# The last token tile in parts of 384 and 128 columns, wv in one transfer, and two stretches of a hand-written order dealt anew

## The chip, the cores and the metric

One core of one Trainium2 chip runs the whole kernel. The metric is device time in microseconds (us) of one execution; several executions are timed and their median is given. Engines are named as the profile names them: PE (TensorE matmul) and PEld (its weight loads), DVE (VectorE), ACT (ScalarE), POOL (GpSimd), SP (SyncE, used here only to issue DMAs).

## The reference

The input x has 2048 tokens of 512 features (bf16). It is normalised, and the result goes through an attention block A and a dense block B; the output is x + A + B.

```python
xn = layernorm(x)                                   # over 512 features, eps 1e-5
# A: 32 heads of 16, the tokens in 4 segments of 512
q, k, v = xn @ wq, xn @ wk, xn @ wv
for s in range(4):
    p = softmax(qs @ ks.T * 16 ** -0.5 + causal mask)    # within the segment
    a_dot = p @ vs
    num, den = phi(qs) @ M, phi(qs) @ z + 1e-6           # phi(t) = t + 1 if t > 0 else exp(t)
    o = g * num / den + (1 - g) * a_dot                  # g = sigmoid(beta), one for each head
    M, z = M + phi(ks).T @ vs, z + sum(phi(ks))          # memory of the segments before
A = concat(o) @ wo
# B
B = silu(xn @ w1) @ w2                              # w1 512 x 1792, w2 1792 x 512
return x + A + B
```

## The kernel before

The tokens stand in 4 segments of 4 tiles of 128. For each tile of the first segment DVE computes sums and variance (`ln_sums`, `ln_var`: words `xc`, `xd`; `xs` is both), ACT the square root (`xq`), DVE its reciprocal (`xi`) and the normalised tile (`Nv`, L315). PE transposes it (`X`, L845), and ACT or DVE copies the transposes to `xnT` (`Xa`, `Xv`, L851). In later tiles the root is taken on POOL (`xg`) and the transposes are made by DMAs that SP issues (`XD`, L857).

The projections are dense products on PE with `xnT`: `k`, `q`, `v`, and `h` for the dense block. A product of a [128, 512] result comes in parts (`v0.0.0` to `v0.0.3` for segment 0, tile 0), each one word. A copy takes the result out of PSUM (`ka`, `kv` and so on: the last letter is the engine). For the scores, k is split into two masked halves (`kf` on ACT and DVE, `kp` on POOL, L385), with masks `pm_odd` and `pm_even` that `odd` makes. `fp`, `fa`, `fv` are the steps of phi on POOL, ACT and DVE, `t` transposes phi(k) by a DMA.

Scores and exponentials go in 72 batches (`S0` to `S71`, in an order of their own: S0, S2, S1, S3, S4, S7, S5, S11, S6, S8, S9, S10, S13 are the first thirteen). One batch fills one PSUM tile `psS` of 2048 columns (L724), one ACT instruction takes the exponential to `Pb` (L730), and POOL sets the masked ones to zero (L744, "select"). `E` and `O` multiply `Pb` with v for the even and odd halves of the heads (L791). PE is a queue: what stands between two batches is worked off there while ACT runs the exp.

What runs when is set by the string `ORDER`: each word calls one function, which issues its instructions at once on their engines, so that the order of the words is the order on each engine. Semaphores between engines follow from the data. The four PSUM banks for projections and outputs are handed out in the order in which they come free.

For outputs, `out_mm` sums for one token tile the 14 products with w2 and the 4 with wo (words `o`; `oc` and `od` do half or a quarter of the columns), and `st` adds x on DVE (`o_out`, L621) and stores it. The very last token tile is summed in two column halves of its own (words `oh`, L338), and each half is added and stored by `half_store` (`sh`, `o_half`, L668 and L672), half 1 first.

The loads at the start: SP issues x tiles, wv (two transfers of 256 KB), wk, wq, more of x, w1; ACT issues two x tiles (L158).

Of the kernel before, what the change touches and what calls it, by code (L numbers as in the profile page):

```python
# [10 lines left out]
BF16 = mybir.dt.bfloat16  # L11
# [4 lines left out]
ORDER = """
ones0 ones1 zeros xc0 xd0 xc1 xq0 xi0 Nv0 busy44 xd1 xq1 xc2 busy6 xi1 X0.1 xd2 xq2 Nv1 X1.1 Xa0.1 v0.0.0 v0.0.1 v0.0.2 xs3 xi2 Nv2 xq3 xi3 v0.0.3 X2.1 Xa1.1 k0.1.0 tb Nv3 X3.1 Xv2.1 k0.1.1 Xv3.1 vv0.0 odd omask k0.0.0 k0.0.1 k0.0.2 k0.0.3 ka0.0 fp0.0 q0.0.0 kf0.0 q0.0.1 q0.0.2 q0.0.3 k0.1.2 k0.1.3 q0.2.0 v0.2.0 qa0.0 xs5 ka0.1 kp0.1
S0 v0.1.0 v0.1.1 xs6 xs7 q0.2.1 v0.2.1 v0.2.2 v0.2.3 vv0.2 fa0.0 k0.2.0 k0.2.1 k0.2.2 xs4 xg4.4
S2 q0.2.2 q0.2.3 qv0.2 k0.2.3 kv0.2 fa0.2 v0.1.2 v0.1.3 vv0.1 Nv5 Nv6 XD6 q0.1.0 q0.1.1 q0.1.2 q0.1.3 Nv7 qv0.1
S1 h0.0.0 h0.0.1 h0.0.2 fp0.2 xs10 h0.0.3 v0.3.0 v0.3.1 v0.3.2 v0.3.3 ha0.0 vv0.3 q0.3.0 hv0.0  # L20
S3 h0.3.0 h0.3.1 q0.3.1 kp0.2 q0.3.2 h0.3.2 tanh XD5 XD7 q0.3.3 h0.3.3 k0.3.0 qv0.3 k0.3.1 xs8 ha0.3
S4 Nv4 h0.1.0 k0.3.2 h0.1.1 hv0.3 XD4 h0.2.0 h0.2.1 h0.2.2 h0.2.3 ha0.2 xs9 k0.3.3 kv0.3 hv0.2
S7 xs11 xg8.4 v1.2.0 v1.2.1 v1.2.2 v1.2.3 vv1.2 h0.1.2 h0.1.3 ha0.1 E0
S5 h0.4.0 h0.4.1 hv0.1 Ev0 h0.4.2 h0.4.3 v1.1.0 v1.1.1 fv0.2 v1.1.2 v1.3.0 fp0.3 ha0.4 v1.1.3 vv1.1
S11 hv0.4 q1.2.0 q1.2.1 q1.2.2 v1.3.1 kind fa0.1 q1.2.3 qv1.2 v1.3.2 v1.3.3 vv1.3 Nv8 XD8 O0 lw0 fv0.0 Ov0
S6 fa0.3 k1.2.0 k1.2.1 k1.2.2 h0.5.0 h0.5.1 h0.5.2 q1.1.0 h0.5.3 ha0.5 kp0.3 k1.2.3 kv1.2 q1.1.1 q1.1.2 hv0.5
S8 h0.7.0 q1.1.3 qv1.1 h0.6.0 h0.6.1 h0.6.2 h0.6.3 ha0.6 kp1.2 fv0.3 E1 Ev1 k1.0.0
S9 hv0.6 h0.7.1 h0.7.2 h0.7.3 Om0 ha0.7 k1.0.1 k1.0.2 q1.0.0 q1.0.1 fp0.1 Nv9 XD9 k1.0.3 q1.0.2 kv1.0 kp1.0
S10 h0.8.0 hv0.7 xs12 h0.8.1 h0.8.2 h0.8.3 ha0.8 h0.9.0 h0.9.1 q1.0.3 t0.3 qv1.0 Nv10 XD10 h0.9.2 h0.9.3
# [64 lines left out]
def kernel(  # L94
# [23 lines left out]
    L = S // NSEG  # L118
    TPS = L // P
# [11 lines left out]
    work = ctx.enter_context(tc.tile_pool(name="work", bufs=2))  # L131
# [21 lines left out]
    wv_sb = cpool.tile([P, DT, D], BF16, name="wv_sb")  # L153
# [14 lines left out]
    def load_w(eng, w_sb, W, k0, k1):  # L168
        eng.dma_start(out=w_sb[:, k0:k1, :], in_=W.rearrange("(ko ki) n -> ki ko n", ki=P)[:, k0:k1, :])
# [45 lines left out]
    kind = cpool.tile([P, 1], F32, name="kind")  # L215
# [16 lines left out]
    omask = cpool.tile([P, 1], I32, name="omask")  # L232
# [100 lines left out]
    def product(out, lhsT, rhs, start, stop):  # L333

        if not narrow[0]:
            return [nc.tensor.matmul(out, lhsT=lhsT, rhs=rhs, start=start, stop=stop, skip_group_check=True)]  # L336
        return [
            nc.tensor.matmul(  # L338
                out[c : c + 32], lhsT=lhsT[:, c : c + 32], rhs=rhs, start=start, stop=stop,
                tile_position=(0, c), skip_group_check=True,  # L340
            )
            for c in range(0, P, 32)
        ]
# [171 lines left out]
    LAST = NSEG - 1  # L515
# [112 lines left out]
    def out_mm(s, j, i, half=None, part=0, parts=1):  # L628

        st = sts[s]  # L630
        width = D if half is None else D // 2
        first = 0 if half is None else half * width
        key = (j,) if half is None else (j, half)
        done = st.setdefault(("done", *key), [])
        if not done:
            assert parts == 1
            if s < LAST or j < 2:
                st["psO", *key] = bank([P, D], F32, "psO")[:, :]
            else:
# [12 lines left out]
        if s == LAST and j >= 2:  # L652
            for other, out in fin_out:
                if other != key:
                    for mm in mms:
                        tc.declare_no_dep(mm.ins, out.ins, reason="the outputs lie in banks of their own")

    fin_out = []

    def half_out(i, h):  # L660
        out_mm(LAST, TPS - 1, i, h)

    def half_store(h):
# [4 lines left out]
        out = nc.vector.scalar_tensor_tensor(  # L668
            out=o_half, in0=st["psO", j, h], scalar=0.5, in1=st["x", j][:, cols], op0=ALU.mult, op1=ALU.add
        )  # L670
        fin_out.append(((j, h), out))
        nc.sync.dma_start(out=out_flat[(NT - 1) * P : NT * P, cols], in_=o_half)  # L672
# [270 lines left out]
```

## Time and profile before

| | |
|---|---|
| median of 3 runs | 220.25 us (219.59, 220.25, 220.25) |
| profiled execution, its own time | 219.92 us |
| its span | 218.2 us |
| busy: PE, ACT, DVE, POOL | 210.5, 184.2, 179.0, 126.8 us |
| share of PE in the chain that ended last | 92% |
| granted TensorE clock | 1.0 over the whole span |

The span is what the profiler sees from the first instruction to the last; the execution's own time is 1.7 us longer. Rows of the timeline give the start in us, the duration, the engine, the line and the operation, how many were joined in the row, and in brackets the idle time ahead and what ended it. Matmuls overlap, so the distance between starts tells what one costs, not its duration.

### The profile page before, as it was taken

How to read it: one execution, taken by the hardware profiler on the slowest of the kernel's cores; microseconds unless marked ns; L12 is line 12 of the kernel's file. 1: busy time of each engine (PE TensorE's matmuls, PEld its weight loads, DVE VectorE, ACT ScalarE, POOL GpSimd, SP SyncE). 2: the span in 40 equal slices, each digit the busy share in tenths (PEclk: the TensorE clock that was granted, in tenths of full speed). 3: DMA queues.
4: the chain of work that ended last, by engine and by line, in shares of the span. 5: the costliest groups of instructions: out<-in, count | busy, mean ns of one | idle time of the engine just before them, and what ended most of it. 6: DMA issues, size and time to landing. Idle time of an engine off the chain costs nothing.

```text
span 218.2 us, 9261 instructions
## 1 busy us (share of the span) xinstructions
PE 210.5 (96%) x3979; PEld 115.0 (53%) x4003; DVE 179.0 (82%) x370; ACT 184.2 (84%) x173; POOL 126.8 (58%) x203
## 2 busy tenths in 40 slices
PE   7899999999999999999999999999999999999994
PEld 7566656655644544444444545445454544465663
DVE  5899999999799879557989886887878897868753
ACT  3799999999999999999999999999989998942000
POOL 6066868969568973886766436963786373410000
PEclk9999999999999999999999999999999999999999
DMA  5995348322203222442125131420042120412322
GB/s 179 357 373 152 51 110 258 62 66 53 51 5 99 75 63 39 99 79 52 49 70 81 54 96 28 74 74 9 0 131 76 48 75 13 133 34 80 91 77 75
DMA packets 33273, 19.60 MB, mean 90 GB/s; under 512 B 14672, under 2 KB 33232, under 8 KB 33232
## 3 DMA queue, kind: packets, MB, share of 16 engines
q1 hardware_dynamic: 30608, 16.39, 28.7%
q10 hardware_dynamic: 2624, 2.62, 3.8%
q8 instruction: 31, 0.51, 1.0%
q14 instruction: 10, 0.08, 0.1%
HBM read 9.96 MB, written 2.10 MB: 55 GB/s over the span
## 4 chain that ended last, share of the span: by engine, by line
PE 92%; DVE 2%; ACT 2%; DMA 1%; issue 1%
PE ps L336 26%; PE psO L338 16%; PE ps L338 16%; PE psS L724 11%; PE psO L336 9%; PE psV L791 8%; PE psS L338 4%; ACT Pb L730 2%; DMA x_lo<-in_A_x_dram 1%; DVE stats L286 1%; PE psM L452 1%; PE ptr L845 0%; DVE xn_t L315 0%; PE ps L509 0%; DVE odd L828 0%
## 5 line engine op out<-in xcount | busy, mean ns | idle before, releaser
L730 ACT ACTIVATE Pb<-psS 128x2048 bf16<-128x2048 f32 x72 | 135.2, 1878 | 4.5 <-PE psS L724 2.2
L744 POOL TENSOR_SCALAR_AFFINE_SELECT Pb<-Pb 128x512 bf16<-128x512 bf16 (+2 forms) x88 | 62.1, 715 | 22.1 <-ACT Pb L730 19.2
L497 DVE SCALAR_TENSOR_TENSOR hT<-th,ps 128x512 bf16<-128x512 bf16 x56 | 38.0, 682 | 11.0 <-ACT th L492 10.6
L744 POOL TENSOR_SCALAR_AFFINE_SELECT lows<-Pb 64x512 bf16<-64x512 bf16 (+1 forms) x40 | 22.9, 572 | 32.5 <-ACT Pb L730 24.2
L338 PE MATMUL psO<-w_sb,hT 128*32 128x512 bf16 (+2 forms) x692 | 41.0, 320 | 0.0
L336 PE MATMUL ps<-xnT,w_sb 128*128 128x512 bf16 (+1 forms) x177 | 36.1, 330 | 0.4 <-DVE pk L433 0.2
L492 ACT ACTIVATE th<-ps 128x512 bf16<-128x512 f32 x56 | 33.0, 593 | 3.7 <-PE ps L338 3.3
L338 PEld LDWEIGHTS <-hT 128*32 128x32 bf16 x860 | 21.4, 96 | 14.5 <-issue 3.1
L338 PE MATMUL ps<-xnT,w_sb 128*32 128x512 bf16 (+1 forms) x408 | 24.6, 349 | 0.0
L724 PE MATMUL psS<-qT,k 32*128 32x64 bf16 (+3 forms) x512 | 23.0, 233 | 0.2
L336 PEld LDWEIGHTS <-w_sb 128*128 128x128 bf16 x178 | 16.4, 98 | 12.0 <-issue 1.2
L336 PE MATMUL psO<-w_sb,hT 128*128 128x512 bf16 (+2 forms) x83 | 20.6, 325 | 0.6 <-issue 0.5
L791 PEld LDWEIGHTS <-Vz 128*32 128x32 bf16 x768 | 16.0, 97 | 9.5 <-issue 0.6
L791 PE MATMUL psV<-Pb,Vz 128*32 128x448 bf16 (+7 forms) x512 | 20.9, 286 | 0.0
L724 PEld LDWEIGHTS <-k 32*128 32x128 bf16 x512 | 9.3, 92 | 21.5 <-issue 20.3
L724 PE MATMUL psS<-qT,kT 16*128 16x448 bf16 (+3 forms) x256 | 14.7, 269 | 0.0
L336 PE MATMUL ps<-xnT,wk_sb 128*128 128x256 bf16 (+1 forms) x63 | 14.1, 326 | 0.2
L336 PEld LDWEIGHTS <-hT 128*128 128x128 bf16 x93 | 8.5, 98 | 9.7 <-issue 2.1
L338 PEld LDWEIGHTS <-w_sb 128*32 128x32 bf16 x408 | 9.9, 96 | 6.6 <-issue 1.5
L828 DVE CAST odd<-psV 128x512 bf16<-128x512 f32 x16 | 11.0, 686 | 2.6 <-PE psV L791 2.4
L399 DVE CAST qT<-ps 128x512 bf16<-128x512 f32 x15 | 10.3, 687 | 3.4 <-PE ps L336 1.8
L338 PE MATMUL psO<-wo_sb,oT 128*32 128x512 bf16 x140 | 12.8, 380 | 0.0
(112 smaller groups left out, 326.7 us busy)
## 6 DMA issues: line engine op xcount, KB each, us to landing
spr<-rz SPq DMA_DIRECT2D x56, 64.0 KB
x_res<-in_A_x_dram SPq DMA_DIRECT2D x16, 128.0 KB
out_dram<-o_out SPq DMA_DIRECT2D x15, 128.0 KB
w_sb<-in_B_w_dram SPq DMA_DIRECT2D x2, 896.0 KB
w_sb<-in_B_w_dram ACTq DMA_DIRECT2D x1, 1792.0 KB
x_hi<-in_A_x_dram SPq DMA_DIRECT2D x2, 512.0 KB
wv_sb<-in_A_wv_dram SPq DMA_DIRECT2D x2, 256.0 KB
wk_sb<-in_A_wk_dram SPq DMA_DIRECT2D x1, 512.0 KB
```

Of the source, the lines that this page charges most:

```text
L286: nc.vector.bn_stats(out=stats[t][:], in_=xs(t, t + 1)[:, 0, :])
L336: return [nc.tensor.matmul(out, lhsT=lhsT, rhs=rhs, start=start, stop=stop, skip_group_check=True)]
L338: nc.tensor.matmul(out[c : c + 32], lhsT=lhsT[:, c : c + 32], rhs=rhs, start=start, stop=stop, tile_position=(0, c), skip_group_check=True,)
L399: copy(out=seg_tile(s, "qT")[:, dt, :], in_=sts[s].pop(("q", dt))[:, :])
L452: nc.tensor.matmul(psM[32 * g : 32 * g + 32, i, :].rearrange("p (r d) -> p r d", d=DH), lhsT=st["phiK", dt][:, j, 32 * g : 32 * g + 32], r ...
L492: nc.scalar.activation(out=th[:], in_=sts[s]["h", ft][:, :], func=AF.Tanh, scale=0.5)
L497: nc.vector.scalar_tensor_tensor(out=st["hT"][:, ft, :], in0=st.pop(("th", ft))[:], scalar=1.0, in1=st.pop(("h", ft))[:, :], op0=ALU.add, ...
L724: nc.tensor.matmul(psS[:, g, c : c + q2 - q1], lhsT=keys[rows], rhs=st["qT"][rows, dt, q1:q2], start=True, stop=True, tile_position=(32 * ...
L730: exp = nc.scalar.activation(out=blocks(Pb, b).rearrange("p y g c -> p g y c"), in_=psS[:, :, :].rearrange("p g (y c) -> p g y c", c=BLOCK ...
L744: over[id(Pb)].append(nc.gpsimd.affine_select(out=out, in_=in_, compare_op=ALU.is_ge, fill=0.0, base=base, pattern=[[0, out.shape[1]], [1, ...
L791: nc.tensor.matmul(psV[32 * g : 32 * g + 32, q0 : q0 + nq].rearrange("p (y c) -> p y c", y=weights.shape[2]), lhsT=Vzs[s % 2][:, kt, 4 * d ...
L828: copy(out=odd[:], in_=sts[s].pop(("psV", 1))[:, :])
```

## The change

Three things. `wv` is loaded by one transfer of 512 KB instead of two of 256 KB. The last token tile's columns are cut at 128 instead of 256: part 1 has 384 columns and is stored first, part 0 has 128 and is stored last. And the words of `ORDER` are dealt anew in two stretches: from the start up to the thirteenth batch (S13), and behind the sixtieth; the words in between stay, and the set of words is the same.

```diff
 ORDER, head
-ones0 ones1 zeros xc0 xd0 xc1 xq0 xi0 Nv0 busy44 xd1 xq1 xc2 busy6 xi1 X0.1 xd2 xq2 Nv1 X1.1 Xa0.1 v0.0.0 v0.0.1 v0.0.2 xs3 ...
+ones0 ones1 zeros odd xc0 xd0 xc1 busy6 xq0 xi0 xd1 xc2 busy44 Nv0 xq1 xd2 xq2 X0.1 xi1 Xa0.1 xs3 v0.0.0 v0.0.1 Nv1 X1.1 ...
...
 ORDER, sixth batch
-S7 xs11 xg8.4 v1.2.0 v1.2.1 v1.2.2 v1.2.3 vv1.2 h0.1.2 h0.1.3 ha0.1 E0
+S7 h0.4.0 hv0.2 h0.4.1 h0.1.3 v1.2.1 v1.2.2 XD4 v1.2.3 kp0.2 E0 xs11 XD7 xg8.4 ha0.1
...
 ORDER, end
-... oh17.1 oh14.1 oh15.1 o3.1.16 o3.1.13 oh2.1 oh1.1 sh1 o3.1.8 oh17.0 oh16.0 st3.1 oh13.0 oh6.0 oh2.0 oh1.0 oh3.0 oh14.0 sh0
+... o3.1.16 o3.1.13 o3.1.8 o3.1.15 st3.1 oh14.1 oh15.1 oh2.1 oh16.1 oh1.1 sh1 oh15.0 oh4.0 oh10.0 oh17.0 oh16.0 oh13.0 oh6.0 oh2.0 oh1.0 oh3.0 oh14.0 sh0

-    load_w(nc.sync, wv_sb, A_wv, 0, 2)
-    load_w(nc.sync, wv_sb, A_wv, 2, 4)
+    load_w(nc.sync, wv_sb, A_wv, 0, 4)
...
 def out_mm(s, j, i, half=None, part=0, parts=1):
-        width = D if half is None else D // 2
-        first = 0 if half is None else half * width
+        first, width = (0, D) if half is None else LAST_COLS[half]
...
+    LAST_COLS = [(0, P), (P, D - P)]
...
 def half_store(h):
-        st, j, cols = sts[LAST], TPS - 1, slice(h * D // 2, (h + 1) * D // 2)
+        (first, width), st, j = LAST_COLS[h], sts[LAST], TPS - 1
+        cols = slice(first, first + width)
...
-        o_half = work.tile([P, L], BF16, name="o_half", tag="pos")[:, 0 : D // 2]
+        o_half = work.tile([P, L], BF16, name="o_half", tag="pos")[:, 0:width]
```

In rows of instructions, line numbers of the changed kernel are smaller by one or two. In the head, DVE's queue up to the third square root's reciprocal stands as follows; `stats` are the sums of one x tile, `mv_all` mean and variance, `rstd_all` the reciprocal root, `xn_t` the normalised tile. Before:

```order
L286 BN_STATS stats<-x_lo 128x6
L289 BN_AGGR mv_all<-stats 128x2
L286 BN_STATS stats<-x_lo 128x6
L306 RECIPROCAL rstd_all<-rstd_all 128x1
L315 TENSOR_SCALAR xn_t<-x_lo,mv_all,rstd_all 128x512
L289 BN_AGGR mv_all<-stats 128x2
L286 BN_STATS stats<-x_lo 128x6
L306 RECIPROCAL rstd_all<-rstd_all 128x1
L289 BN_AGGR mv_all<-stats 128x2
L315 TENSOR_SCALAR xn_t<-x_lo,mv_all,rstd_all 128x512
L286 BN_STATS stats<-x_lo 128x6
L289 BN_AGGR mv_all<-stats 128x2
```

DVE's same place in the changed kernel, from the mask reductions on:

```order
L221 TENSOR_REDUCE pm_odd<-b_112 128x1
L222 TENSOR_REDUCE pm_even<-b_112 128x1
L284 BN_STATS stats<-x_lo 128x6
L287 BN_AGGR mv_all<-stats 128x2
L284 BN_STATS stats<-x_lo 128x6
L304 RECIPROCAL rstd_all<-rstd_all 128x1
L287 BN_AGGR mv_all<-stats 128x2
L284 BN_STATS stats<-x_lo 128x6
L313 TENSOR_SCALAR xn_t<-x_lo,mv_all,rstd_all 128x512
L287 BN_AGGR mv_all<-stats 128x2
L304 RECIPROCAL rstd_all<-rstd_all 128x1
L284 BN_STATS stats<-x_lo 128x6
```

The third statistics now stand ahead of the first normalisation, and the fourth ahead of the second; the mask reductions come first.

POOL's queue between the fourth batch's select and the sixth's: `Pb` and `lows` are the selects, `k_463` (`k_583` after) the split k of the third group, `pos` a step of phi. Before:

```order
L744 AFFINE_SELECT Pb_144<-Pb_144 128x1024
L417 TENSOR_SCALAR pos<-kT 128x512
L744 AFFINE_SELECT Pb_145<-Pb_145 128x4x64 x2
L385 TENSOR_SCALAR k_463<-kT,pm_odd 128x4x128
L385 TENSOR_SCALAR k_463<-kT,pm_even 128x4x64
L744 AFFINE_SELECT lows<-Pb_146 64x512
L744 AFFINE_SELECT Pb_146<-Pb_146 128x8x128
L744 AFFINE_SELECT Pb_147<-Pb_147 128x512
L297 TENSOR_SCALAR rstd_all<-mv_all 128x4
```

POOL's same place after:

```order
L743 AFFINE_SELECT Pb_144<-Pb_144 128x4x64 x2
L415 TENSOR_SCALAR pos<-kT 128x512 x2
L743 AFFINE_SELECT lows<-Pb_145 64x512
L743 AFFINE_SELECT Pb_145<-Pb_145 128x8x128
L743 AFFINE_SELECT Pb_146<-Pb_146 128x512
L383 TENSOR_SCALAR k_583<-kT,pm_odd 128x4x128
L383 TENSOR_SCALAR k_583<-kT,pm_even 128x4x64
L295 TENSOR_SCALAR rstd_all<-mv_all 128x4
```

The split k has moved behind the selects of the fifth and the sixth batch, and a second `pos` stands ahead of them.

At the end of the program, SP's queue holds the last stores. Before:

```order
L614 DMA x_res<-in_A_x_dram 128x512
L626 DMA out_dram<-o_out 128x512 x2
L672 DMA out_dram<-o_half 128x256
L626 DMA out_dram<-o_out 128x512
L672 DMA out_dram<-o_half 128x256
```

SP's same place after:

```order
L612 DMA x_res<-in_A_x_dram 128x512 x2
L624 DMA out_dram<-o_out 128x512
L612 DMA x_res<-in_A_x_dram 128x512
L624 DMA out_dram<-o_out 128x512 x3
L671 DMA out_dram<-o_half 128x384
L671 DMA out_dram<-o_half 128x128
```

The last whole tile's store has moved ahead of the first part's, so the two parts come last, one behind the other. DVE's last instructions have the same order as these stores.

More of the change, by code (lines that the diff above doesn't have):

```diff
@@ L13 @@
 I32 = mybir.dt.int32
[L16 to L19, printed above, removed]
@@ new lines @@
+S0 xs4 k0.2.0 xs7 fa0.0 v0.1.0 k0.2.1 xs5 v0.2.2 v0.2.3 q0.2.1 vv0.2 q0.2.2 q0.2.3 xs6 k0.2.2 xg4.4
+S2 k0.2.3 kv0.2 v0.1.1 q0.1.0 v0.1.2 q0.1.1 qv0.2 q0.1.2 q0.1.3 v0.1.3 h0.3.0 fa0.2
+S1 v0.3.0 qv0.1 v0.3.1 vv0.1 v0.3.2 v0.3.3 Nv6 h0.0.0 h0.0.1 Nv7 h0.0.2 h0.0.3 ha0.0 q0.3.0
+S3 q0.3.1 h0.3.1 Nv5 fp0.2 vv0.3 xs10 hv0.0 h0.2.0 h0.3.2 Nv4 q0.3.2 q0.3.3 h0.3.3 h0.2.1 fp0.0 ha0.3 k0.3.0
+S4 k0.3.1 qv0.3 k0.3.2 h0.1.0 XD6 k0.3.3 h0.2.2 h0.1.1 xs9 h0.1.2 h0.2.3 hv0.3 ha0.2 kv0.3 xs8 XD5 v1.2.0
+S7 h0.4.0 hv0.2 h0.4.1 h0.1.3 v1.2.1 v1.2.2 XD4 v1.2.3 kp0.2 E0 xs11 XD7 xg8.4 ha0.1
@@ new lines @@
+S5 h0.4.2 vv1.2 h0.4.3 ha0.4 v1.1.0 Ev0 hv0.1 v1.1.1 v1.1.2 tanh v1.1.3 q1.2.0 q1.2.1 kind vv1.1 v1.3.0
+S11 v1.3.1 v1.3.2 q1.2.2 hv0.4 q1.2.3 v1.3.3 fv0.2 fa0.1 fp0.3 O0 vv1.3 qv1.2 h0.5.0
+S6 h0.5.1 h0.5.2 k1.2.0 Ov0 fv0.0 k1.2.1 q1.1.0 kp0.3 h0.5.3 k1.2.2 ha0.5 q1.1.1 k1.2.3 Nv10
+S8 q1.1.2 kv1.2 h0.6.0 h0.6.1 q1.1.3 h0.7.0 fp0.1 kp1.2 fa0.3 hv0.5 h0.6.2 h0.6.3 E1 h0.7.1 ha0.6 qv1.1
+S9 Nv8 k1.0.0 k1.0.1 h0.7.2 k1.0.2 Ev1 h0.7.3 q1.0.0 q1.0.1 q1.0.2 fv0.3 t0.3 hv0.6 ha0.7 k1.0.3 Nv9 XD8 kv1.0 kp1.0
@@ L30 @@
+S10 h0.8.0 XD9 h0.8.1 h0.8.2 q1.0.3 h0.9.0 h0.9.1 h0.9.2 hv0.7 h0.8.3 lw0 xs12 h0.9.3 ha0.8 qv1.0 Om0 XD10
 S13 hv0.8 O1 Ov1 xs15 v1.0.0 v1.0.1 v1.0.2 ha0.9 v1.0.3 vv1.0 h0.10.0 h0.10.1 bmask
@@ L83 @@
 S64 nv2.3 od2.0.6.3 o2.2.4 od2.0.6.2 hv3.8 o2.2.14 dv2.1 h3.9.0 h3.9.1 o2.2.9 od2.2.13.1 ha3.9 s3 sv3 o2.2.17 hv3.9 r3.3
-S68 o2.0.14 zv2.1 h3.5.0 h3.5.1 n2.1 z2.2 nv2.1 Om13 ha3.5 o2.0.12 o2.0.2 o2.0.3
+S68 o2.0.14 od2.2.13.0 zv2.1 h3.5.0 h3.5.1 n2.1 z2.2 nv2.1 Om13 ha3.5 o2.0.12 o2.0.2 o2.0.3
 S65 oc2.0.13.1 o2.2.2 hv3.5 o2.1.13 oc2.1.0.0 oc2.1.3.0 zv2.2 od2.1.9.0 o2.1.4 o2.0.8 o2.0.17 dv2.2 E14 oc2.1.3.1 Ea14
-S66 o2.1.10 od2.2.13.0 o2.1.17 o2.1.6 o2.2.15 n2.2 r3.2 Om12 oc2.2.1.1 o2.1.12 o2.1.5 o2.1.11 o2.0.15 r3.1 r3.0 w3 d3.3 d3.0
+S66 o2.1.10 o2.1.17 o2.1.6 o2.2.15 n2.2 r3.2 Om12 oc2.2.1.1 o2.1.12 o2.1.5 o2.1.11 o2.0.15 r3.1 r3.0 w3 d3.3 d3.0
```

12 lines of the change are left out of this document (2 added, 10 removed).

## The prediction

> **What bounds the kernel.** I read the busy table and the windows first, then the waits of PE (TensorE), and only then the three places that the change touches: the head, the stretch up to the thirteenth score batch, the tail. All durations are from the profiled execution: span 218.2 us, its own time 219.92 us. The median of the runs shown is 220.25 us, 0.33 above it (0.15%), and the lowest run is 219.59. So a difference worked out below is set against 219.92, and compared with both.
>
> The first fence has one line of the busy table, the windows (busy time of each engine in each stretch), the exp group of ACT (ScalarE) between 12.3 and 41.4 us (its last number is the idle time ahead of it), and the largest wait of PE.
>
> ```profile
> PE 210.5 (96%) x3979; PEld 115.0 (53%) x4003; DVE 179.0 (82%) x370; ACT 184.2 (84%) x173; POOL 126.8 (58%) x203
> core 0: us, PE busy (x) PEld busy (x) DVE busy (x) ACT busy (x) POOL busy (x), PEclk, DMA share, GB/s
> 5.40:8.43 3.03, 1.90 (x16) 1.00 (x18) 2.92 (x12) 1.88 (x7) 0.00 (x0) 1.00 1.03 348
> 8.43:11.90 3.47, 3.47 (x34) 2.69 (x32) 2.77 (x9) 3.17 (x7) 0.77 (x1) 1.00 1.09 369
> 11.90:41.30 29.40, 29.00 (x430) 18.31 (x435) 28.35 (x63) 29.01 (x27) 21.57 (x35) 1.00 0.59 167
> 41.30:175.00 133.70, 132.00 (x2586) 66.44 (x2605) 111.84 (x225) 130.18 (x116) 92.12 (x140) 1.00 0.27 62
> L730 ACT ACTIVATE Pb<-psS 128x2048 bf16<-128x2048 f32 x12 | 22.5, 1877 | 0.4
> PE ptr L845 <- DVE xn_t L315: 1.1, 2, 0.8
> ```
>
> PE is the bound. It is busy for 210.5 of 218.2 us. In the 29.40 us up to the thirteenth batch it works for 29.00, so no order of the same work can win more than 0.40 us there; in the 133.70 us after it, which keep their order, it works for 132.00. The one stretch with real idle time is 5.40 to 8.43: 1.90 of 3.03 us, 1.13 idle, of which 1.1 is the wait of the transposes for the normalised tiles. That 1.13 and that 0.40, with a tail in which PE has already stopped, are all that this change can touch. ACT comes second up to the thirteenth batch: 29.01 of 29.40, and ahead of its twelve exps it stands idle for only 0.4. A batch there can therefore also be held by ACT, and I come back to that.
>
> **wv in one transfer.** This removes one DMA issue on SP (the DMA queue of SyncE).
>
> ```profile
> 3.22 0.51 SPq L169 DMA_DIRECT2D wq_sb<-in_A_wq_dram  x1
> 3.64 0.69 DVE L286 BATCH_NORM_STATS2 stats<-x_lo 128x6 f32<-128x512 bf16 x1 [1.01 <-DMA x_lo<-in_A_x_dram]
> 4.47 0.66 DVE L286 BATCH_NORM_STATS2 stats<-x_lo 128x6 f32<-128x512 bf16 x1
> 4.65 0.29 ACT L303 ACTIVATE rstd_all<-mv_all,eps 128x1 f32<-128x1 f32 x1 [1.44 <-DVE mv_all L289]
> 5.04 0.14 DVE L306 RECIPROCAL rstd_all<-rstd_all 128x1 f32<-128x1 f32 x1
> 5.23 0.41 DVE L315 TENSOR_SCALAR xn_t<-x_lo,mv_all,rstd_all 128x512 bf16<-128x512 bf16 x1
> 5.65 0.66 DVE L286 BATCH_NORM_STATS2 stats<-x_lo 128x6 f32<-128x512 bf16 x1
> 5.70 0.40 PE L845 MATMUL ptr<-ident,xn_t 128*128 128x128 bf16 x4 [0.30 <-DVE xn_t L315]
> 6.44 0.38 DVE L315 TENSOR_SCALAR xn_t<-x_lo,mv_all,rstd_all 128x512 bf16<-128x512 bf16 x1
> 6.56 0.29 ACT L303 ACTIVATE rstd_all<-mv_all,eps 128x1 f32<-128x1 f32 x1 [0.50 <-DVE mv_all L289]
> 6.76 0.63 ACT L851 COPY xnT<-ptr 128x256 bf16<-128x256 bf16 x2
> 6.88 0.40 PE L845 MATMUL ptr<-ident,xn_t 128*128 128x128 bf16 x4 [0.79 <-DVE xn_t L315]
> 7.17 1.04 PE L336 MATMUL ps<-wv_sb,xnT 128*128 128x512 bf16 x3
> 7.87 0.63 ACT L851 COPY xnT<-ptr 128x256 bf16<-128x256 bf16 x2
> 8.43 0.38 PE L336 MATMUL ps<-xnT,wk_sb 128*128 128x256 bf16 x2
> 8.95 1.27 PE L336 MATMUL ps<-xnT,wk_sb 128*128 128x256 bf16 x10
> 10.06 1.04 PE L336 MATMUL ps<-xnT,wq_sb 128*128 128x256 bf16 x8
> 11.91 0.21 PE L724 MATMUL psS<-qT,k 32*128 32x64 bf16 x4
> ```
>
> An issue costs about 0.5 us of SP (wq's row), so wk, wq and the next x leave some 0.5 us earlier. Nobody waits for them: neither the first wk product (8.43) nor the first wq product (10.06) shows a wait for a DMA, and in the new order they start at about 8.77 and 10.29 (below). The bytes ahead of them stay the same. The first wv product starts at 7.17 and now needs the whole of wv where it needed a half. The whole was there by the third of those products, 7.17 + 2 x 0.22 = 7.6 at the latest, and PE reaches the first at 7.14; with the transfer one issue earlier at its end I put this at 0, with 0.2 as the loss if wv lands late, and 0 as the gain: the work that hides wk and wq is the chain of normalised tiles, and if that went faster they would have to land before 8.4, which they did.
>
> **The head's order on DVE (VectorE).** Two short mask reductions go ahead of the first statistics, into the idle time before 3.64. The third statistics (0.66, at 5.65 before) go ahead of the first normalisation (at 5.23 before). Working it forward with these durations: the first reciprocal keeps 5.04, the second aggregate follows, the third statistics take 5.25 to 5.83 if the third x tile has landed, and the first normalised tile starts at 5.83, 0.60 later. Its transposes on PE go from 5.70 to 6.30. Their copy on ACT was at 6.76, though, behind the square root at 6.56. That root now runs at 6.37, since its aggregate comes earlier, and the copy at 6.73: the first wv product comes at 7.14 against 7.17. So the 0.60 is absorbed there. The second normalised tile goes from 6.44 to 7.13, its transposes from 6.88 to 7.60; PE does two of the four wv products ahead of them and two behind (to 8.27), then the other transposes (8.27 and 8.53). The copy for wk ends near 8.66 and the first wk product comes at 8.77 instead of 8.43. Before, PE had done two wk products by 8.95 and went on with ten; after, it does all twelve from 8.77 without a break, at 0.109 each (half of the 0.22 of 512 columns), to 10.07. Then come one product of wv for the third token tile (0.22, to 10.29), the eight wq products (0.87, to 11.16), and two wk pieces, one wv piece and one wq piece (4 x 0.218, to 12.03), then 0.10 for the q copy: the first score batch starts at 12.13 instead of 11.91. Of these 0.22 us, 0.218 is a wv piece that stood behind the first batch and now stands ahead of it. The head is worth 0.00 net, with PE idle for about 0.1 us more in it and that same tenth won by leaving out the gaps of the old order.
>
> Bounds: if the transposes came without any wait, the 1.13 would be won. That is excluded in part, since normalisation, transposes and copies remain a chain: the most I see is half of it, -0.5. On the other side the new order makes the first normalisation wait for the third x tile. Before, the statistics of that tile started at 5.65 with no wait shown, so it may have landed at any time up to then; if only at 5.65, everything moves by 0.40. I take 0.00 because the row gives no wait, and keep -0.5 and +0.4.
>
> **Up to the thirteenth batch.** The pieces are the same; they are dealt out to other batches. Each batch has a score product (0.4 us), an exp (1.88) and some nine product pieces of 0.218 on PE.
>
> ```profile
> 21.96 1.88 ACT L730 ACTIVATE Pb<-psS 128x2048 bf16<-128x2048 f32 x1
> 23.73 0.59 ACT L492 ACTIVATE th<-ps 128x512 bf16<-128x512 f32 x1
> 24.34 1.88 ACT L730 ACTIVATE Pb<-psS 128x2048 bf16<-128x2048 f32 x1
> 26.71 1.88 ACT L730 ACTIVATE Pb<-psS 128x2048 bf16<-128x2048 f32 x1
> 22.41 0.83 POOL L385 TENSOR_SCALAR k<-kT,pm_odd 128x512 bf16<-128x512 bf16 x1
> 23.22 0.48 POOL L385 TENSOR_SCALAR k<-kT,pm_even 128x256 bf16<-128x256 bf16 x1
> 23.97 0.66 POOL L744 TENSOR_SCALAR_AFFINE_SELECT lows<-Pb 64x512 bf16<-64x512 bf16 x1 [0.28 <-ACT Pb L730]
> ```
>
> Here two exps follow at the closest: 21.96, 24.34, 26.71, or 2.37 to 2.38 us, which is ACT's own limit; the mean over the twelve is 29.40/12 = 2.45. In the new order one piece less stands here (-0.218, already counted in the head), and two batches, the sixth and the eighth, hold only six pieces beside a weighing (about 2.28 us on PE) and are held by ACT at 2.376: 2 x 0.09 = 0.18 of waiting. The old order had about 0.28 of such waits inside its 0.40 idle. The stretch becomes 29.40 - 0.218 - 0.28 + 0.18 + 0.04 (a long chain of ACT work in the tenth) = 29.12, and the thirteenth batch stands at 12.13 + 29.12 = 41.25 instead of 41.30: -0.05. I take -0.03, since the sums of pieces are only good to a few hundredths. Bounds: -0.30 if the waits go altogether, +0.2 from POOL (GpSimd). That engine split the k of the third head group at 22.41 and 23.22 (1.31 us) in an idle gap ahead of the mask at 23.97. In the new order this split stands behind the mask of the sixth batch, at about 27.2 to 28.6, and the eighth batch needs it at about 28.9. I price the move at 0, because 0.3 us remain; what hides it is the two batches between, and if the masks run 0.5 late, PE waits 0.2.
>
> The move of one output quarter from the batch named S66 to S68, two batches earlier, is 0.055 us of PE work that stays on PE: 0.
>
> **The tail.** The last token tile's sum came in halves of 256; now 384 columns are finished first, then 128. The three rows of SP are the last three stores; L621 and L668 are the sums on DVE.
>
> ```profile
> 214.37 0.72 PE L338 MATMUL psS<-w_sb,hT 128*32 128x256 bf16 x20
> 214.50 0.68 DVE L621 SCALAR_TENSOR_TENSOR o_out<-psO,x_res 128x512 bf16<-128x512 f32 x1
> 214.61 0.33 SPq L672 DMA_DIRECT2D out_dram<-o_half  x1
> 214.91 0.28 PE L338 MATMUL psS<-wo_sb,oT 128*32 128x256 bf16 x4
> 215.20 0.33 SPq L626 DMA_DIRECT2D out_dram<-o_out  x1
> 215.25 0.42 DVE L668 SCALAR_TENSOR_TENSOR o_half<-psS,x_res 128x256 bf16<-128x256 f32 x1
> 215.70 0.33 SPq L672 DMA_DIRECT2D out_dram<-o_half  x1
> ```
>
> PE's work stays: twenty products of 256 columns, four side by side, fill 214.37 to 214.91, so 0.108 for four, half the 0.22 of 512 columns; 384 and 128 columns together take what two 256s take (estimate from these rows). On DVE, 512 columns take 0.68 and 256 take 0.42, a line of 0.16 + 0.26 per 256: 128 columns take about 0.29, 0.13 less. That is the gain if the last sum alone sets the end: it would end at 215.54 instead of 215.67. But the full tile's store and the 384-column store are now issued right ahead of it. DVE ends the one at about 214.50, the other at 215.19; SP issues at 214.52 and 215.21, each 0.33, and with about 0.1 us between two issues (215.20 to 215.70 is 0.50 with 0.33 busy) it is free at about 215.6. So the last issue comes at 215.57 to 215.65 against 215.70: -0.05 to -0.13. I take -0.08. After that issue, 2.5 us pass until the span's end (218.2), and I keep them, though the transfer has half the bytes: before, the first half's store and the last were also of one size and nothing here shows a smaller one. From below: if half the bytes saved half a transfer, some -0.1 more; from above: +0.25, if rows of 256 bytes land later than rows of 512.
>
> The Trainium skill, "DMA: Bandwidth & Descriptors", section Specifications, names 512 bytes as the smallest transfer at full rate, with a read-modify-write below it. The last store's rows go from 512 to 256 bytes, so by this rule the gain of the tail would be lost or reversed; by the rows alone it is -0.08. No transfer with 256-byte output rows stands in this trace, so it can't be weighed here before the run; it is rival three below.
>
> **Sum.** 0.00 (wv) + 0.00 (head) - 0.03 (middle) - 0.08 (tail) = -0.11 us: 219.8 against the profiled execution, 220.1 against the median. I take 220.0. About 0.3% (0.66 us) is what a measurement of this kernel can tell from no change, and the sum is a sixth of that.
>
> **Rivals.**
> 1. *Faster: the head's waits go.* If the third x tile lands by 5.2, and the new order lets PE pass from transposes to products with half of its 1.13 idle, and the waits for ACT go as well (-0.3), the time is 220.0 - 0.5 - 0.3 = 219.2. For it: PE can use every tenth it is given. Against it: the second normalised tile comes 0.69 later, and PE has only four wv products (0.87) to fill that gap with. 0.23.
> 2. *Slower: the first normalisation waits for x.* The third statistics stand ahead of it on DVE, so the landing of the third x tile now stands in the chain, and behind it the transposes, the first wv products and all of PE's work. From a landing of 5.25 on, each tenth is a tenth of the time. At 5.65, the last moment that the row allows, it is +0.40, 220.4, still no change. It decides from 6.15 on (+0.9, 220.9), and at 6.3 gives 221.05: the tile would have to come 0.5 to 0.65 later than it can have come before, because the whole wv, now one transfer of 512 KB issued ahead of it, takes its turn. For it: the tile is only known to be there by 5.65. Against it: the bytes under way are the same, and no wait is shown at 5.65. 0.13.
> 3. *The tail gives nothing:* the 256-byte rows land later, or SP's three issues end when they did. 220.0 + 0.08 to + 0.33: 220.1 to 220.3, still no change. Most of that lies inside the forecast, so I set it apart only for its price: 0.12.
> 4. *The middle does the opposite* (the k split on POOL late by 0.2, ACT ties of 0.3 more): 220.5, also inside 0.3%. 0.05.
>
> The forecast itself, a time within a few tenths of before, has 0.47. Cases inside 0.3% are the forecast, three and four: 0.47 + 0.12 + 0.05 = 0.64 same. Faster is rival one, 0.23; slower is rival two, 0.13. The range must leave out 0.2: its low end is rival one with most of its gain, 219.2, and its high end is the tile at 5.65 and the tail's bound together, +0.4 and +0.25, with most of the +0.2 of a late split on POOL: 220.8.
>
> **What would show it.** Right: in the profile after, the first normalised tile near 5.83 and the second near 7.13; the first wv product at 7.1 to 7.2; the first score batch at 12.1; the thirteenth at 41.2 to 41.3; the last sum on DVE of about 0.29 us and the last store issued near 215.6. Wrong: statistics on DVE that wait for an x tile with the first normalised tile after 6.0; wv products later than 7.4 (wv's landing); a wait of PE for POOL's k in the eighth batch; more than 2.6 us from the last issue to the end of the span. A first batch at 11.7 or earlier would be rival one.

## The result and the profile after

The change made the kernel slower: 222.84 us (median of 5, 222.35 to 223.37) against 220.25 (219.59 to 220.32), a ratio of 1.0119 with a 95% interval of 1.0098 to 1.0139. The forecast was 220.0 in a range of 219.2 to 220.8.

The profiled execution took 222.35 us, its span is 220.6. First its page, with PE's busy time and the bytes moved, in 40 slices of 5.5 us each; the last line is that of the kernel before, for the same row.

```profile
PE 211.1 (96%) x3988; PEld 114.6 (52%) x4012; DVE 179.6 (81%) x370; ACT 184.6 (84%) x173; POOL 126.0 (57%) x203
GB/s 175 334 375 157 60 4 4 161 226 124 74 4 73 82 43 54 96 102 51 48 51 88 50 91 22 71 76 33 0 103 74 76 74 2 107 66 75 72 99 77
```

```profile
GB/s 179 357 373 152 51 110 258 62 66 53 51 5 99 75 63 39 99 79 52 49 70 81 54 96 28 74 74 9 0 131 76 48 75 13 133 34 80 91 77 75
```

PE's busy time grew by 0.6 us only, so most of the 2.4 us are waits. In the transfers something has moved: the 258 GB/s that stood in the seventh slice before (33 to 38 us) are gone, and 161, 226 and 124 stand in the eighth to the tenth (39 to 55 us). A large load runs later.

The starts of some score batches on PE (the rows of the scores' line) tell where the time goes:

| | before | after | difference |
|---|---|---|---|
| first batch | 11.91 | 12.79 | +0.88 |
| thirteenth | 41.30 | 41.91 | +0.61 |
| seventeenth | 50.91 | 53.30 | +2.39 |
| twenty-eighth | 78.38 | 81.02 | +2.64 |
| last | 189.81 | 192.46 | +2.65 |
| end of the span | 218.2 | 220.6 | +2.4 |

So there are four pieces: +0.88 at the start, -0.27 up to the thirteenth batch, +1.78 in the four batches behind it, whose words did not change, +0.26 near 80 us, and at the end about -0.2.

The rows of the timeline for the largest one, in the changed kernel: ACT issues the load of w2 (L168), SP issues transposes of xn and of phi(k), PE multiplies with the transposed phi(k) (`psM`), ACT takes the exps of the sixteenth and the seventeenth batch. The second fence is a step of the chain that ended last, the third has the same places before.

```profile
39.96 0.39 ACTq L168 DMA_DIRECT2D w_sb<-in_B_w_dram  x1
40.17 4.31 SPq L856 DMA_TRANSPOSE xnT<-xn_t  x3
45.69 1.43 SPq L439 DMA_TRANSPOSE phiK<-pk  x1
49.54 1.88 ACT L729 ACTIVATE Pb<-psS 128x2048 bf16<-128x2048 f32 x1
52.73 0.37 PE L450 MATMUL psM<-Vz,phiK 128*32 128x32 bf16 x32 [1.18 <-DMA phiK<-pk]
53.74 1.88 ACT L729 ACTIVATE Pb<-psS 128x2048 bf16<-128x2048 f32 x1 [1.78 <-PE psS L723]
```

```profile
45.69 6.99 DMA phiK<-pk
```

```profile
44.54 1.19 SPq L441 DMA_TRANSPOSE phiK<-pk  x1
50.34 0.40 PE L452 MATMUL psM<-Vz,phiK 128*32 128x32 bf16 x32
51.36 1.88 ACT L730 ACTIVATE Pb<-psS 128x2048 bf16<-128x2048 f32 x1
```

The transpose of phi(k) was issued at 45.69 and PE got it at 52.7, 7 us later; before, it was issued at 44.54 and PE used it at 50.34 with no wait shown. PE waits 1.18 us for it, the scores behind it in PE's queue start late, and ACT stands idle for 1.78 us. The bytes moved between 28 and 54 us, in 40 slices of 0.65 us, show what the transposes met. After, and then before:

```profile
GB/s 0 0 3 3 25 0 0 0 0 2 4 0 0 0 25 0 3 3 67 134 58 175 277 383 329 377 294 211 253 353 290 52 10 223 231 284 246 73 6 3
```

```profile
GB/s 0 0 3 85 134 225 370 378 372 310 362 367 323 142 15 0 3 3 53 162 51 151 0 81 146 3 4 147 55 142 73 0 98 129 3 3 3 3 0 92
```

Before, the load of w2 (1792 KB) ran from 30 to 37 us. After, its packets run from 41 to 50 us, beside the four transposes shown above. The traffic by queue shows what that meant. Three transposes of xn had been issued from 40.17 on. From 41 to 44 us, ACT's queue (q10: packets, MB, share of the time of 16 DMA engines), which carries the load, and SP's (q1), which carries the transposes, moved in the changed kernel:

```profile
q10 hardware_dynamic: 696, 0.71, 81.9%
q1 hardware_dynamic: 6, 0.00, 0.1%
```

With the load issued early and the same order of transposes, issued from 39.57 on (the second experiment below), SP's queue moved in the same 3 us:

```profile
q1 hardware_dynamic: 1386, 0.34, 57.4%
```

So the transposes stood nearly still beside the load. What the row above shows from 49.5 to 52 us (223 to 284 GB/s) is, but for 0.06 MB, SP's queue. The word `lw0` that issues the load went from the eighth batch's list to the twelfth's. The prediction does not speak of it.

The start of the changed kernel, with the two normalised tiles, the first wv product and the first score batch:

```profile
5.54 0.40 DVE L313 TENSOR_SCALAR xn_t<-x_lo,mv_all,rstd_all 128x512 bf16<-128x512 bf16 x1
6.80 0.38 DVE L313 TENSOR_SCALAR xn_t<-x_lo,mv_all,rstd_all 128x512 bf16<-128x512 bf16 x1
7.88 0.38 PE L334 MATMUL ps<-wv_sb,xnT 128*128 128x512 bf16 x1 [1.49 <-DMA wv_sb<-in_A_wv_dram]
12.79 0.21 PE L723 MATMUL psS<-qT,k 32*128 32x64 bf16 x4
```

Both tiles came 0.3 earlier than forecast (5.83 and 7.13), and yet the first wv product starts at 7.88 and not at 7.14: it waited for wv.

### The profile page after: what moved, and what is told of

Its sections match the earlier page's. It is cut to its first block, busy times and chain, and to the rows that moved or that the text cites. A ratio compares the mean times of both kernels' runs of the same rounds, so it can differ in the third digit from the quotient of the medians.

```text
span 220.6 us, 9280 instructions
## 1 busy us (share of the span) xinstructions
PE 211.1 (96%) x3988; PEld 114.6 (52%) x4012; DVE 179.6 (81%) x370; ACT 184.6 (84%) x173; POOL 126.0 (57%) x203
## 4 chain that ended last, share of the span: by engine, by line
PE 86%; DMA 6%; DVE 4%; issue 1%; SPq 1%
PE ps L334 25%; PE psO L336 16%; PE ps L336 14%; PE psS L723 10%; PE psO L334 9%; PE psV L790 7%; PE psS L336 4%; DMA phiK<-pk 3%; DMA wv_sb<-in_A_wv_dram 3%; DVE phiQT L431 1%; PE psM L450 1%; DVE odd L827 1%; DVE qT L397 1%; DVE stats L284 1%; DVE hT L495 1%
## 5 line engine op out<-in xcount | busy, mean ns | idle before, releaser
L334 PE MATMUL ps<-xnT,w_sb 128*128 128x512 bf16 (+1 forms) x171 | 35.6, 332 | 0.4 <-DVE pk L431 0.2
L336 PEld LDWEIGHTS <-hT 128*32 128x32 bf16 x860 | 20.8, 96 | 14.9 <-issue 3.1
L336 PE MATMUL ps<-xnT,w_sb 128*32 128x512 bf16 (+1 forms) x432 | 25.8, 344 | 0.0
L383 POOL TENSOR_SCALAR k<-kT,pm_odd 128x512 bf16<-128x512 bf16 x15 | 10.8, 721 | 10.1 <-ACT kT L374 9.1
L334 PE MATMUL ps<-xnT,wk_sb 128*128 128x256 bf16 (+1 forms) x64 | 14.8, 327 | 0.1
L336 PEld LDWEIGHTS <-w_sb 128*32 128x32 bf16 x432 | 10.7, 96 | 6.4 <-issue 1.7
L334 PE MATMUL ps<-wv_sb,xnT 128*128 128x512 bf16 x37 | 11.4, 380 | 1.9 <-DMA wv_sb<-in_A_wv_dram 1.5
```

Source lines behind the costliest of these rows:

```text
L336: nc.tensor.matmul(out[c : c + 32], lhsT=lhsT[:, c : c + 32], rhs=rhs, start=start, stop=stop, tile_position=(0, c), skip_group_check=True,)
L383: nc.gpsimd.tensor_scalar(out=to, in0=frm, scalar1=keep[:, 0:1], scalar2=1.0, op0=ALU.mult, op1=ALU.mult)
```

## The experiments

The theories: L, that w2's load, issued at 40 us, holds up the transposes; W, that the single wv transfer lands late for its first product. Their rivals: Q and S, that the three xn transposes in a row in SP's queue do it; H, that the start's loads were late for another reason; M, that a late w2 costs by itself, because something needs it. The ratios are to the kernel before, run on the same chip beside each.

**wv in two transfers again** (the changed kernel otherwise).

```diff
-    load_w(nc.sync, wv_sb, A_wv, 0, 4)
+    load_w(nc.sync, wv_sb, A_wv, 0, 2)
+    load_w(nc.sync, wv_sb, A_wv, 2, 4)
```

> The changed kernel with wv in two transfers again; all else as changed. Theory W (the single transfer lands late as a whole, and the first product needs all of it): the first wv product comes at about 7.1 to 7.2 us instead of 7.88, the first score batch at about 12.1 instead of 12.79, and the time falls by 0.7 to 0.9, from 222.8 to 222.0. Rival H (the loads at the start land late for another reason, the order of the work on DVE and SP or plain scatter of the memory): the wv product still waits for a DMA, and the time stays within 0.3 of 222.8. Either way the wait for the transposed phi(k) near 51 us stays, about 1.8 us.

222.25 us, ratio 1.0088 (1.0063 to 1.0113). The first wv product and PE's wait for phi(k):

```profile
7.26 0.61 PE L335 MATMUL ps<-wv_sb,xnT 128*128 128x512 bf16 x2 [0.46 <-ACT xnT L851]
53.12 0.38 PE L451 MATMUL psM<-Vz,phiK 128*32 128x32 bf16 x32 [1.43 <-DMA phiK<-pk]
```

The wait for the wv transfer is gone; what is left is a wait for the copy of the transposes on ACT. The first batch starts at 12.19, near the forecast 12.13. The median fell by 0.6, less than the 0.7 to 0.9 expected, while the wait for phi(k) became a little longer (1.43). The interval overlaps that of the changed kernel, so the 0.6 alone is not clear of scatter.

**w2's load where it was** (the changed kernel otherwise).

```diff
-S11 ... fp0.3 O0 vv1.3 qv1.2 h0.5.0
+S11 ... fp0.3 O0 lw0 vv1.3 qv1.2 h0.5.0
-S10 ... hv0.7 h0.8.3 lw0 xs12 h0.9.3 ha0.8 qv1.0 Om0 XD10
+S10 ... hv0.7 h0.8.3 xs12 h0.9.3 ha0.8 qv1.0 Om0 XD10
```

> The changed kernel with the load of w2 (word lw0, 1792 KB) issued behind the eighth batch's O0 as before, not in the twelfth batch; all else as changed. Theory L (the w2 transfer, moved from 29 to 40 us, fills the DMA engines while the transposes of xn and of phi(k) wait behind it): PE's wait for phiK near 51 us, 1.18 us, goes, the exps of the 16th and 17th batch are 2.4 apart instead of 4.2, and the time falls by 1.8, from 222.8 to 221.0. Rival Q (three xn transposes in a row stand ahead of phi(k)'s in SP's queue): the wait stays at over 1 us, the time within 0.4 of 222.8.

220.13 us, ratio 1.0004 (0.9985 to 1.0024): 2.7 us less than the changed kernel, more than the 1.8 expected of one profile (one of its twelve runs took 222.21). The first wv product and the product with phi(k):

```profile
6.97 0.59 PE L334 MATMUL ps<-wv_sb,xnT 128*128 128x512 bf16 x2 [0.56 <-DMA wv_sb<-in_A_wv_dram]
50.34 0.40 PE L450 MATMUL psM<-Vz,phiK 128*32 128x32 bf16 x32
```

No wait for phi(k), with SP's queue and its three transposes in a row unchanged: Q is out. The first wv product waits 0.56 us for its transfer here.

**Both edits.**

> Both of the two edits. If W and L are both right and add up: 222.8 - 0.8 - 1.8 = 220.2, the time of before (220.25) within 0.4, with the tail's small gain and the 0.3 that the new order won between the first and the thirteenth batch left over (219.9). Under H and Q together it stays near 222.8; under L alone 221.0; under W alone 222.0.

219.76 us, ratio 0.9990 (0.9976 to 1.0003). Alone, the two edits won 0.6 and 2.7 us; together they win 3.1, which is all that was lost. The windows from 41.30 to 53.30 us, of the changed kernel and of this one (length, then PE busy):

```profile
41.30:53.30 12.00, 10.71 (x271) 5.99 (x270) 10.38 (x22) 10.59 (x10) 10.03 (x16) 1.00 1.06 222
```

```profile
41.30:53.30 12.00, 11.99 (x285) 6.48 (x273) 11.61 (x25) 11.86 (x11) 10.02 (x16) 1.00 0.39 59
```

PE was busy for 10.71 of 12 us and is now busy for 11.99; the transfers there fell from 222 to 59 GB/s. Run again (below), this kernel gave 219.83.

**wv in one transfer, in the kernel before.**

> The kernel before with wv in one transfer, nothing else changed. Theory W: the first wv product waits for the DMA, 7.17 becomes 7.6 to 7.9, and the time rises by 0.4 to 0.8, to 220.7 to 221.0; less than in the changed kernel if two of its four products no longer stand ahead of the second transposes. Rival H: no wait for a DMA, time 220.25 within 0.3.

220.16 us, ratio 0.9997 (0.9980 to 1.0013). A miss: the wait for the wv transfer is there, but the time does not change.

```profile
7.47 1.02 PE L335 MATMUL ps<-wv_sb,xnT 128*128 128x512 bf16 x4 [0.37 <-DMA wv_sb<-in_A_wv_dram]
```

0.37 us is waited, and the four wv products then run behind each other. The first batch starts at 12.33 in this profile, within the 11.91 to 12.69 of the three profiles with the old head and two transfers. That the 1.13 us of idle time in the old order hide the wait is likely, but not shown.

**w2's load late, in the kernel before**, the one word moved.

```diff
-S11 ... XD8 O0 lw0 fv0.0 Ov0
+S11 ... XD8 O0 fv0.0 Ov0
-S10 h0.8.0 hv0.7 xs12 h0.8.1 h0.8.2 h0.8.3 ha0.8 ...
+S10 h0.8.0 hv0.7 xs12 h0.8.1 h0.8.2 h0.8.3 lw0 ha0.8 ...
```

> The kernel before with one word moved: the load of w2 in the twelfth batch's list (behind its h0.8.3) instead of the eighth's. Theory L: this alone costs what the change lost there; PE waits for the transposed phi(k) near 51 us, for 1 to 2.5 us, and the time is 221.5 to 222.7. Rival S (the late w2 hurts only with the new order of the xn transposes, three in a row): no wait, 220.1 within 0.3.

222.97 us, ratio 1.0119 (1.0083 to 1.0154), slower by as much as the whole change. The wait is nearly the same:

```profile
52.36 0.38 PE L452 MATMUL psM<-Vz,phiK 128*32 128x32 bf16 x32 [1.07 <-DMA phiK<-pk]
```

S is out as well: one word makes this kernel as slow.

**w2's load later still** (the changed kernel with wv in two transfers, `lw0` in the fifteenth batch's list, behind `ha1.0`).

> The changed kernel with wv in two transfers, and w2's load issued still later, in the fifteenth batch's list (near 49 us), behind the transposes of phi(k) that PE waited for. Theory L (what hurts is that the w2 packets stand ahead of these transposes in the DMA engines): the wait near 51 us goes although w2 comes later, 219.8 to 220.3, against 222.25 with w2 in the twelfth batch. If the transposes of the other phi(k) half (issued near 53 us, needed at about 62) are held in turn, up to 1 us is lost again. Rival M (the kernel needs w2 early, lateness itself costs): 222.3 or more, with a wait for w2 on PE.

225.23 us, ratio 1.0220 (1.0196 to 1.0244). The expected cure did not come, and the run shows the mechanism best. The wait for phi(k) has gone, since its transposes went ahead of the load. But the last xn transpose of that stretch, issued 0.4 us behind the load, now met it:

```profile
47.72 0.39 ACTq L168 DMA_DIRECT2D w_sb<-in_B_w_dram  x1
48.11 1.21 SPq L857 DMA_TRANSPOSE xnT<-xn_t  x1
50.54 0.40 PE L451 MATMUL psM<-Vz,phiK 128*32 128x32 bf16 x32
57.62 0.13 PEld L335 LDWEIGHTS <-wk_sb 128*128 128x128 bf16 x2 [4.01 <-DMA xnT<-xn_t]
57.63 1.03 PE L335 MATMUL ps<-xnT,wk_sb 128*128 128x512 bf16 x2 [3.73 <-DMA w_sb<-in_B_w_dram]
```

The weight load of the k projection waited 4.01 us for the transposed xn. (For the matmul itself the row names the w2 transfer, but its operands are xnT and wk; what ends such a wait is inferred, and w2's last packets came at 57.1.) From 49 to 52 us, with that transpose issued, SP's queue moved no packet and ACT's 0.83 MB. Rival M forecast a time like this one, but with PE waiting for w2. The product that waited does not read w2, and the first that does starts at 70.9 us, so M is out. The windows of this stretch show a second loss (PEclk is the column behind POOL's):

```profile
core 0: us, PE busy (x) PEld busy (x) DVE busy (x) ACT busy (x) POOL busy (x), PEclk, DMA share, GB/s
53.80:57.63 3.83, 0.10 (x5) 0.01 (x1) 1.53 (x4) 2.49 (x3) 2.21 (x5) 0.95 0.92 188
57.63:61.20 3.57, 3.57 (x18) 1.86 (x22) 0.80 (x2) 0.00 (x0) 0.00 (x0) 0.57 0.26 63
```

After 3.83 us of idle PE, its granted clock was 0.57 for the next 3.57 us. So 3.7 us of wait became 5.3 us at the start of the nineteenth batch (61.17; 5.48 behind that of before, 0.20 of it there earlier). From 61.2 us on the clock was 1.00 again. In the changed kernel, the wait of 1.2 us left it at 1.00. The Trainium skill, "TensorE: Matmul & The Clock Gate", Part 1, says that a window of about 3.4 us without work halves the clock, until about as long a busy one; both stretches here agree.

**The tail alone, in the kernel before** (columns 384 and 128, and the three lists behind the sixtieth batch).

> The kernel before with the new tail alone: columns 384 and 128, and the three lists behind the sixtieth batch. Forecast of the prediction: -0.08 us, from an earlier last store, 220.0. Rival (256-byte rows land later): 0 to +0.25, with more than 2.6 us from the last issue to the end of the span.

219.96 us, ratio 0.9985 (0.9970 to 1.0000). The forecast of -0.08 lies inside the interval, and so, at its edge, does no change. In its profile 2.5 us pass from the last issue to the end of the span, not the more than 2.6 of the rival.

**The new lists up to the thirteenth batch alone, in the kernel before**, with w2's load and wv as before.

> The kernel before with the new lists up to the thirteenth batch, but w2's load in the eighth batch and wv in two transfers; the tail as before. If the gain of both edits together (219.76 against 220.09, not yet clear of scatter) comes from the order: the thirteenth batch starts at about 41.1 instead of 41.30 and the time is 219.8 to 219.9. If it comes from the tail: 220.1.

220.23 us, ratio 0.9993 (0.9978 to 1.0009): no change that can be told. In the profile the thirteenth batch starts at 41.01 (about 41.1 was expected), 0.29 earlier than in the kernel before; by the twenty-eighth it is 0.04 earlier. The last section shows where the 0.25 between went, in the rows near 74 us:

```profile
74.07 1.10 POOL L743 TENSOR_SCALAR_AFFINE_SELECT Pb<-Pb 128x1024 bf16<-128x1024 bf16 x1
74.10 1.61 DVE L432 SCALAR_TENSOR_TENSOR phiQT<-ex,pos 128x512 bf16<-128x512 bf16 x1
```

**w2's load in two halves** (the changed kernel with wv in two transfers; 896 KB in the eighth batch's list, 896 KB in the twelfth's).

```diff
-        "lw": lambda i: load_w(nc.scalar, *((w2_sb, B_w2, 0, FT), (wo_sb, A_wo, 0, DT))[i]),
+        "lw": lambda i: load_w(nc.scalar, *((w2_sb, B_w2, 0, FT // 2), (wo_sb, A_wo, 0, DT), (w2_sb, B_w2, FT // 2, FT))[i]),
-S11 ... O0 vv1.3 ...
+S11 ... O0 lw0 vv1.3 ...
-S10 ... h0.8.3 lw0 xs12 ...
+S10 ... h0.8.3 lw2 xs12 ...
```

> The changed kernel with wv in two transfers, and w2's load cut in two: 896 KB in the eighth batch's list as before, 896 KB in the twelfth's as in the change. Theory L: how long the DMA engines are full decides. The late half is through after some 5 us, near 45 to 46 us, where the transpose of phi(k) that PE needs near 51 us is only issued: no wait on PE, 219.8 to 220.3. Rival: any load of w2 next to the transposes costs as much, 221.5 to 222.3.

220.18 us, ratio 1.0002 (0.9985 to 1.0019). With half the bytes at the same late place, the product with phi(k) comes without a wait:

```profile
50.38 0.40 PE L451 MATMUL psM<-Vz,phiK 128*32 128x32 bf16 x32
```

The late half's last packet starts at 44.39, and SP issues the transpose of phi(k) at 44.69. So a load at this place is harmless if it is through before that transpose is issued; the three transposes of xn that it did meet cost PE no wait.

**Both edits again, and w2 early alone again**, on one chip.

> The kernel of both edits once more (w2 early, wv in two transfers), beside the next one on the same chip: 219.8 again, ratio to before 0.998 to 0.999 if the gain of a third of a microsecond is real.

> The kernel with w2 early and wv in one transfer once more, beside the one ahead: 0.2 to 0.4 us slower than that (220.0 to 220.2) if one transfer of wv costs what the first comparison gave (220.13 against 219.76); equal within 0.1 if that was scatter of the start.

219.83 (0.9988, interval 0.9975 to 1.0001) and 220.22 (1.0001, 0.9987 to 1.0016). The difference of 0.39 us repeats the 0.37 of the first comparison. In each of the two the intervals overlap, but both lean the same way and by the same amount, so one transfer of wv probably costs some 0.4 us in the new order. How long PE waits for it differs from profile to profile; here the single transfer held the first product longest:

```profile
8.27 0.38 PE L334 MATMUL ps<-wv_sb,xnT 128*128 128x512 bf16 x1 [1.88 <-DMA wv_sb<-in_A_wv_dram]
```

No kernel beats the one before by more than the measurement can tell; the closest are the tail alone (0.9985) and both edits together (0.9990 and 0.9988), with intervals that end at 1.0000 to 1.0003.

## Why the prediction was wrong

**The step that failed first** is the sum's middle term: "The pieces are the same; they are dealt out to other batches", priced by PE, ACT and POOL at -0.03. Among the pieces was `lw0`, the load of 1792 KB on ACT's queue. It wasn't counted as a DMA that moves. Read by the engines that the prediction looked at, the term was good: from the first batch to the thirteenth the forecast was 29.12, and 41.91 - 12.79 is 29.12. It is 29.10 to 29.11 in all nine profiles with the new lists, and 29.39 in the four with the old. What it left out was the DMA engines, and with them the stretch behind the thirteenth batch, which "keep their order" on PE and so was taken as untouched. There the runs showed +1.78 in the profile and, by moving that word alone, +2.7 in the kernel before and -2.7 in the changed one. From the thirteenth batch to the seventeenth it is 11.39, 12.39 and 10.85 us in the three profiles with the whole load in the twelfth batch's list, and 9.61 to 9.62 in the other ten. The Trainium skill, "DMA: Bandwidth & Descriptors", section "Issuing engines are not separate DMA queues", says that transfers from any issuer run on the same 16 DMA engines and interleave. The trace agrees that ACT's load and SP's transposes meet, but the sharing was not even: 0.71 MB against less than 0.01 from 41 to 44 us. Why SP's queue got so little is not shown.

**The wv term** was "0.2 as the loss if wv lands late" and 0 taken. The profile after shows a wait of 1.49 us, of which 0.46 would have gone to ACT's copy in any case (the wait with two transfers), and the first batch starts 0.60 later than with two (12.79 against 12.19). Over the timed runs it costs some 0.4 in the new order and nothing that can be told in the old. The step that failed is the landing: "the whole was there by the third of those products" held for two transfers and was carried over to one. Every profile with one transfer shows a wait for it (1.49, 0.56, 0.37, 1.88 us), none of the nine with two does. The start scatters with two transfers too: the profile of the tail alone, otherwise the kernel before, shows a wait for the next weights,

```profile
PE ps L335 <- DMA wk_sb<-in_A_wk_dram: 0.6, 1, 0.6
```

with its first batch at 12.24 instead of 11.91. So theory H holds a part, and one profile's 0.9 at the start was not the price; the 0.4 of the two timed comparisons is the better estimate. Why the single transfer lands later, by up to a microsecond and differently in each profile, stays open: no run took it apart.

**The head's order** came out near the forecast once wv was split: the first batch starts at 11.90 to 12.39 in the six profiles with the new head and two transfers, 12.13 was forecast. The old head with two transfers gave 11.91 to 12.69 in three, so the 0.22 that the prediction put between the two orders can't be told from the scatter of the start. The third x tile, the second rival's concern, was no issue: the statistics did not wait and both tiles were early.

**The POOL split of k** was priced at 0, and PE's products show no wait for it in the profile after. It was close: the weight load for the eighth batch's scores waited 0.42 us for POOL, at 29.56, while PE still worked on other products.

**The tail** was -0.08, with the last sum at 0.29 and no loss from 256-byte rows. The two last sums on DVE and the last two issues, joined in one row of 0.81 us:

```profile
L667 DVE SCALAR_TENSOR_TENSOR o_half<-psS,x_res 128x384 bf16<-128x384 f32 x1 | 0.6, 558 | 0.1
L667 DVE SCALAR_TENSOR_TENSOR o_half<-psS,x_res 128x128 bf16<-128x128 f32 x1 | 0.3, 292 | 0.1
217.87 0.81 SPq L671 DMA_DIRECT2D out_dram<-o_half  x2
```

The last sum took 292 ns, as worked out. From the start of the last score batch, the last store is issued after 25.89 us in the four profiles with the old tail and after 25.79 in the nine with the new one: 0.10 earlier, within the forecast's 0.05 to 0.13, though the issue itself takes 0.42 us instead of 0.33. From that issue to the end of the span it is 2.38 to 2.52 us with the old tail and 2.38 to 2.57 with the new, so the rows of 256 bytes did not land later in any profile, and that part of rival three is out. From the last batch to the end of the span the mean is 28.36 us with the old tail and 28.26 with the new. The single values overlap (28.27 to 28.40 and 28.17 to 28.36), so a gain of 0.1 fits but is not proven, and the timed runs could not tell it from no change.

**The slower rival** had the right sign and a wrong cause: x for the third tile. It did look at a load that lands late at the start, as wv did, but what decided stood some 40 us further on. That the time came out slower, as this rival had it, was luck.

## What to carry to other kernels

When an order of work is dealt anew, list the large transfers that move with it, with their times under way, before pricing any engine: here 1792 KB at 40 us instead of 29 cost 2.7 us, through transposes that another engine had issued. For each small transfer that an engine will soon wait for (here a transpose), ask what large load will be under way when it is issued, and put the load well ahead of it or cut it into pieces that are through by then. A wait can have its cause more than 10 us ahead of it: the load was issued at 40 us and PE waited at 52. A stretch whose words keep their order isn't untouched by that.

## What the runs showed that was not expected

A DMA transpose that is there at most 5.8 us after its issue (before, issued at 44.54 and used at 50.34 without a wait) takes 7 us from issue to landing with the load beside it (45.69 to 52.69). xn's transpose, issued beside the load in the later placing, held PE until 57.62, 9.5 us after its issue.

The +0.26 near 80 us is no part of the change's plan. Two instructions start there nearly together, a select on POOL and a phi on DVE. In the changed kernel, and then in the kernel before:

```profile
76.74 1.10 POOL L743 TENSOR_SCALAR_AFFINE_SELECT Pb<-Pb 128x1024 bf16<-128x1024 bf16 x1
76.77 1.61 DVE L431 SCALAR_TENSOR_TENSOR phiQT<-ex,pos 128x512 bf16<-128x512 bf16 x1
```

```profile
74.37 1.65 POOL L744 TENSOR_SCALAR_AFFINE_SELECT Pb<-Pb 128x1024 bf16<-128x1024 bf16 x1
74.38 0.68 DVE L433 SCALAR_TENSOR_TENSOR phiQT<-ex,pos 128x512 bf16<-128x512 bf16 x1
```

Where POOL starts 0.03 us ahead, it takes 1.10 and DVE 1.61; where it starts 0.01 ahead, it takes 1.65 and DVE 0.68. One of the two is held by the other. In the thirteen profiles of this study the split is clean: in six, POOL is 0.02 to 0.03 us ahead and DVE takes 1.61 to 1.62; in seven it is less than 0.01 ahead (in one, DVE is first) and DVE takes 0.68. DVE's loss of 0.93 makes the copy of q late: in the changed kernel it ends at 78.99, and PE's next product starts at 79.04. PE's twenty-eighth batch comes 0.26 later (27.72 or 27.73 us behind the seventeenth in five of the six, 27.46 or 27.47 in the seven; in the sixth a longer wait hides it). The two profiles of both edits, one and the same kernel, fall on different sides. So a hundredth or two of a microsecond between two starts moves the time by a tenth of a per cent, and it is no property of the order. That both engines want the same thing is argued from the durations; no run set out to test it.
